# Padding three-row matmuls to 128 rows and shortening a routing step in an FFT and mixture-of-experts kernel

## The chip, the cores and the metric

The kernel runs on one core of a Trainium2 chip. A core has TensorE (PE in the rows; PEld is its weight load), VectorE (DVE), ScalarE (ACT), GpSimd (POOL) and SyncE (SP, which here only issues transfers). The metric is the device time of one execution in microseconds (us), the median over several runs.

## The reference, cut to what matters

```python
X = np.fft.fft(np.fft.fft(x, axis=1), axis=2).real        # x: 8 x 3072 x 256
x = X.reshape(8 * 3072, 256)
h = x @ w_in                                               # 256 -> 2048
g = h * np.clip(h + 3, 0, 6) / 6
x = g @ w_out                                              # 2048 -> 256
logits = x @ w_gate                                        # 8 experts
expert = argmax(logits); gate = softmax(logits)[expert]
out = gate * (relu(x @ w1[expert]) @ w2[expert])           # 256 -> 1024 -> 256
```

## The kernel before, in words

The transform over the 256 columns is folded into `w_in` when the kernel starts, and the one over the 3072 rows is done by folds on VectorE and GpSimd and by matmuls with tables. Because of symmetries, TensorE computes two halves, A and B, of each hidden tile; B - A and A + B are the hidden values of two mirrored sets of tokens. One column of the transform, d = 128, doesn't fit the 128 rows of a matmul. It enters by a matmul of its own with three rows (high part, low part and a cross term), whose weights are in the tile W3 and whose data are in q3.

The first stage has 48 chunks of 512 tokens, each with 8 steps (`step(s)`, 384 in all); a step is two hidden blocks of 128. In a step:

- `mm1` issues 6 matmuls for A, 2 three-row matmuls for d = 128 and 6 for B, into the tile `ab` (two banks; two such tiles take turns).
- `mm2` issues 24 matmuls of the step three before, 16 with gh and 8 with gl, into four banks `acc`.
- `h_of` copies A to SBUF on ScalarE and forms h[0] and h[1] on VectorE. Then come r (ScalarE), r times h (VectorE), gh (ScalarE) and gl (GpSimd) for the hidden values of the step before. r, gh and gl have four buffers of 512 each, two steps' worth.

At a chunk's end ScalarE evacuates acc (`evac`), and `routing` puts its stages into later steps: s0 and s1 find the expert, s2 counts on GpSimd, s3_mm computes the rank of each token by a matmul, s3 turns it into row numbers `pi` on VectorE, and s4 issues four scatters from GpSimd's queue, which write the tokens to DRAM in the order of experts. FFT matmuls of coming groups and folds of the next batch entry are put into the same steps by tables of step numbers. A batch entry has 6 chunks, 48 steps. The framework fixes each engine's order when the kernel is built, and each engine works strictly in its order.

After the first stage (from about 2162 us) the second mixture of experts works on tiles of 512 or 256 sorted tokens. The change doesn't touch that code.

`load_q3` copies rows of the transform to q3 by small SP transfers, three chunk steps before they are used.

Of the kernel before, what the change touches and what calls it, by code (L numbers as in the profile page):

```python
# [22 lines left out]
P = 128  # L23
# [32 lines left out]
QB = 5  # L56
BIG = float(1 << 20)
# [16 lines left out]
def tile_fft_moe(ctx, tc, xr, xf, xcoef, w_in, w_out, w_gate, w1, w2, tabs, fm, misc, tri, sgn8, dstc, maskc, out):  # L74
# [55 lines left out]
    sel1 = pc.tile([P, P], F32R, name="sel1")  # L130
# [7 lines left out]
    base8 = pc.tile([P, 4, NE], F32, name="base8")  # L138
# [191 lines left out]
    def load_q3(ci):  # L330
        b, g, c = chunks[ci]
        pq, o = gt[(b, g)], slice(c * 256, (c + 1) * 256)
        hold["q3", ci] = t = pw.tile([P, 256], F32R, tag="q3", name=f"q3_{ci}")
        v = t.rearrange("(j r) n -> j r n", r=32)
        for r, i in ((0, 2), (1, 2), (2, 3)):
            sp.dma_start(v[:, r].bitcast(F32), pq[0:1, i, None, o].to_broadcast([1, 4, 256]).bitcast(F32))
# [7 lines left out]
    def load_consts():  # L344
# [6 lines left out]
        sp.dma_start(base8, misc[:, o:o + 32].rearrange("p (a c) -> p a c", a=4))  # L351
        o += 32
# [5 lines left out]
    def start_tables():  # L358
        dve.memset(SS0.bitcast(F32), 0.0)
        for t in (XN, sel1):  # L360
            pool.memset(t.bitcast(F32), 0.0)
        dve.memset(half, 0.5)
        dve.memset(onesb, 1.0)
        dve.memset(sel1[0:1, :].bitcast(F32), 1.0)
        dve.memset(cnt, 0.0)

# [81 lines left out]
    def w_in_ev(c):  # L448
# [5 lines left out]
        th = pw.tile([P, 2, P], F32R, tag="Ac", name=f"th{c}")  # L454
        v = ab[:, :, 258:258 + P]
        act.activation(th, v, AF.Copy)
        for i in range(2):
            f = 2 * c + i
            r = slice(f % 4 * 32, f % 4 * 32 + 3)
            dve.scalar_tensor_tensor(out=W3[r, f // 4], in0=th[r, i], scalar=ssel[r, :], in1=v[r, i], op0=ALU.mult, op1=ALU.add)  # L460

# [25 lines left out]
    def mm1(ab, f0, pq, c0, q3):  # L487
        f = [slice((f0 + i) * P, (f0 + i + 1) * P) for i in range(2)]
        for i in range(2):
            for n, (a, c) in enumerate(PASS):  # L490
                pe.matmul(ab[:, i, 0:256], WA[a][:, f[i]], pq[:, c, c0:c0 + 256], start=n == 0, stop=False)  # L491
        for i in range(2):
            r = slice((f0 + i) % 4 * 32, (f0 + i) % 4 * 32 + 3)
            pe.matmul(ab[:, i, 0:256], W3[r, (f0 + i) // 4], q3[r], start=False, stop=True)  # L494
        for i in range(2):
            mm_group(ab[:, i, 256:512], [(WB[a][:, f[i]], pq[:, 2 + c, c0:c0 + 256]) for a, c in PASS])

    def h_of(ab, h, s):
# [47 lines left out]
    def routing(xo, xp, t0, nt, mask, tagn, wait=RKW):  # L546
# [5 lines left out]
        def s0():  # L552
# [4 lines left out]
            st["ex"] = ex = sm("rt_ex", [P, 4, NE])  # L557
            act.activation(ex[:, 0:nt], d[:, 0:nt], AF.Exp)
# [21 lines left out]
        def s3_mm():  # L580
            ab = hold["ride"][:, 1] if hold.get("ride") is not None else bank(f"rk{tagn}")
            st["r"] = r = ab[:, 384:384 + nt * NE]
            mm_group(r, [(trib, st["oh"][:, 0:nt].rearrange("p t e -> p (t e)")),
                         (onesb, st["oc"][:, 0:nt].rearrange("p t e -> p (t e)"))])

        def s3():
            k = st["k"]
            r = st["r"].rearrange("p (t e) -> p t e", e=NE)
            dve.tensor_tensor(out=k[:, 0:nt], in0=base8[:, 0:nt], in1=r, op=ALU.add)
            s = sm("rt_s", [P, 4])  # L590
            dve.tensor_reduce(out=s[:, 0:nt], in_=st["ex"][:, 0:nt], axis=AX.X, op=ALU.add)
# [690 lines left out]
```

## Time and profile before

| | |
|---|---|
| median of 3 runs | 3366.51 us (3363.07 to 3368.29) |
| the profiled execution | 3363.55 us; its span 3361.7 us |
| TensorE busy | 3207.4 us, 95% of the span |
| VectorE, ScalarE, GpSimd busy | 2277.2, 1939.8, 2263.8 us |
| first stage, second stage | about 44 to 2162 us, 2162 to 3361 us |

Matmuls are pipelined, so a busy share near 100% says that TensorE seldom stood still, not that each matmul was as short as it can be. What a matmul costs is read from the distance between starts. Waits name the instruction whose end came last.

### The profile page before, as it was taken

The numbers are of one execution on the slowest core, as the hardware profiler recorded it, in microseconds if no ns is written. First come the engines' busy times: TensorE is split into PE (matmuls) and PEld (weight loads), VectorE is DVE, ScalarE is ACT, GpSimd is POOL, SyncE is SP. The second block draws the span as 40 slices with busy tenths as digits, with TensorE's granted clock in tenths as the row PEclk, the third lists the DMA queues.
The fourth block names the chain that finished last, engine by engine and source line by source line (L and its number), as shares of the span: only waits on it lengthen the run. The fifth ranks groups of instructions, "written<-read, shape, count | busy, mean of one in ns | idle before, by whom it ended". The sixth has DMA issues, their size and how long they took to land.

```text
span 3361.7 us, 62365 instructions
## 1 busy us (share of the span) xinstructions
PE 3207.4 (95%) x23482; PEld 2983.5 (89%) x23482; DVE 2277.2 (68%) x3700; ACT 1939.8 (58%) x3339; POOL 2263.8 (67%) x1781
## 2 busy tenths in 40 slices
PE   5899999999999999999999999999999999999998
PEld 5899999889889889889889999888888888888887
DVE  8877777777777777777777665755555555555543
ACT  3566566566666666666666665645445444445453
POOL 5567776776776777677676775766666656666664
PEclk8999999999999999999999999999999999999999
DMA  5100100100100100000000001065555555555560
GB/s 180 61 28 19 38 24 16 43 24 16 39 27 16 33 33 16 33 31 18 27 14 16 14 16 50 20 180 159 153 151 152 151 146 148 159 147 154 146 170 31
DMA packets 248130, 243.45 MB, mean 72 GB/s; under 512 B 149099, under 2 KB 210956, under 8 KB 247824
## 3 DMA queue, kind: packets, MB, share of 16 engines
q1 hardware_dynamic: 226576, 184.94, 19.7%
q0 software_dynamic: 21248, 54.48, 4.5%
q8 instruction: 187, 3.06, 0.4%
q14 instruction: 119, 0.97, 0.1%
HBM read 159.71 MB, written 54.04 MB: 64 GB/s over the span
## 4 chain that ended last, share of the span: by engine, by line
PE 60%; ACT 13%; DVE 13%; issue 6%; POOL 2%; DMA 0%; SPq 0%; ACTq 0%; DVEq 0%; POOLq 0%
PE acc L517 16%; PE op L164 16%; PE hp L164 15%; PE ab L164 5%; ACT gh L961 5%; ACT r L505 5%; PE ab L491 4%; DVE h L183 2%; PE ab L494 2%; DVE r L512 1%; DVE R L188 1%; DVE R L180 1%; POOL gl L183 1%; DVE H L180 1%; DVE H L188 1%
## 5 line engine op out<-in xcount | busy, mean ns | idle before, releaser
L183 POOL TENSOR_TENSOR gl<-r,gh 128x512 fp32r<-128x512 f32 x768 | 1108.0, 1462 | 486.1 <-ACT gh L961 371.5
L505 ACT ACTIVATE r<-h,half 128x512 f32<-128x512 f32 x768 | 546.3, 719 | 590.3 <-DVE h L183 375.3
L512 DVE SCALAR_TENSOR_TENSOR r<-r,h 128x512 f32<-128x512 f32 x768 | 621.1, 813 | 363.2 <-ACT r L505 362.0
L517 PE MATMUL acc<-WO,gh 128*128 128x264 f32 x6144 | 822.7, 287 | 4.0 <-ACT xo L536 4.0
L517 PEld LDWEIGHTS acc<-WO,gh 128*128 128x128 f32 x6144 | 784.8, 191 | 4.2 <-ACT xo L536 4.2
L997 DVE SCALAR_TENSOR_TENSOR WB<-hp,WA 128x512 fp32r<-128x512 f32 (+1 forms) x472 | 278.8, 606 | 302.7 <-ACT WA L996 302.6
L961 ACT ACTIVATE gh<-r 128x512 fp32r<-128x512 f32 x768 | 450.9, 622 | 41.5 <-PE acc L517 14.7
L517 PE MATMUL acc<-WO,gl 128*128 128x264 f32 x3072 | 440.1, 285 | 0.5 <-POOL gl L183 0.5
L491 PE MATMUL ab<-pq,WA 128*128 128x256 f32 x2304 | 344.3, 285 | 64.2 <-DVE h L180 33.0
L517 PEld LDWEIGHTS acc<-WO,gl 128*128 128x128 f32 x3072 | 403.2, 189 | 0.9 <-POOL gl L183 0.9
L164 PE MATMUL ab<-pq,WB 128*128 128x256 f32 x2304 | 383.6, 303 | 0.0
L491 PEld LDWEIGHTS ab<-pq,WA 128*128 128x128 f32 x2304 | 300.6, 189 | 73.2 <-issue 53.9
L996 ACT ACTIVATE WA<-hp 128x512 fp32r<-128x512 f32 (+1 forms) x472 | 241.4, 531 | 197.6 <-PE hp L164 194.6
L164 PEld LDWEIGHTS ab<-pq,WB 128*128 128x128 f32 x2304 | 302.2, 192 | 50.4 <-issue 1.6
L148 POOL DMA_INDIRECT out_dram<-yo,dst x200 | 217.4, 1087 | 155.7 <-DVE yo L1097 117.7
L148 POOL DMA_INDIRECT xs_dram<-xp,pic x192 | 212.3, 1106 | 122.1 <-DVE pic L603 66.2
L164 PE MATMUL hp<-xTb,TB 128*128 128x512 f32 (+1 forms) x1344 | 277.3, 364 | 13.5 <-DVE WB L997 13.5
L164 PE MATMUL hp<-xTa,W1b 128*128 128x512 f32 (+1 forms) x1392 | 277.3, 358 | 3.2 <-DVE WB L997 3.2
L164 PEld LDWEIGHTS hp<-xTb,TB 128*128 128x128 f32 x1344 | 225.7, 188 | 57.8 <-DVE WB L997 15.3
L164 PE MATMUL op<-W2b,WA 128*128 128x256 f32 x1536 | 276.4, 282 | 0.0
L183 DVE TENSOR_TENSOR h<-A,ab 128x512 f32<-128x512 f32 x384 | 259.9, 677 | 22.1 <-ACT A L500 21.6
L164 PEld LDWEIGHTS hp<-xTa,W1b 128*128 128x128 f32 x1392 | 228.9, 189 | 44.4 <-DVE WB L997 3.6
(268 smaller groups left out, 5328.0 us busy)
## 6 DMA issues: line engine op xcount, KB each, us to landing
w1a<-in_w_dram SPq DMA_DIRECT2D x29, 1024.0 KB
w1b<-in_w_dram SPq DMA_DIRECT2D x29, 1024.0 KB
w2b<-in_w_dram SPq DMA_DIRECT2D x58, 512.0 KB
R<-in_xr_dram SPq DMA_DIRECT2D x32, 774.0 KB
w2a<-in_w_dram SPq DMA_DIRECT2D x29, 768.0 KB
w2d<-in_w_dram SPq DMA_DIRECT2D x28, 256.0 KB
raw<-in_w_in_dram SPq DMA_DIRECT2D x8, 512.0 KB
rawo<-in_w_out_dram SPq DMA_DIRECT2D x8, 512.0 KB
```

The lines of the kernel that those rows point to most:

```text
L148: i = pool.indirect_dma_start(oob_is_err=False, **kw)
L164: pe.matmul(dst, l, r, start=(n == 0), stop=(n == len(terms) - 1))
L180: pinned(eng.tensor_tensor(out=o, in0=a, in1=b, op=ALU.add))
L183: i = eng.tensor_tensor(out=o, in0=a, in1=b, op=ALU.subtract)
L188: pinned(dve.scalar_tensor_tensor(out=o, in0=a, scalar=s, in1=b, op0=ALU.mult, op1=ALU.add))
L491: pe.matmul(ab[:, i, 0:256], WA[a][:, f[i]], pq[:, c, c0:c0 + 256], start=n == 0, stop=False)
L505: act.activation(r, h, AF.Relu, bias=half, scale=1.0 / 6.0)
L512: dve.scalar_tensor_tensor(out=g, in0=r, scalar=1.0, in1=h, op0=ALU.min, op1=ALU.mult)
L517: pe.matmul(acc[t][:, 0:GW], lhs, wo(w, f0 + i), start=st, stop=sp_)
L961: act.activation(gh[n], g[n], AF.Copy)
L996: act.activation(hi, ps, AF.Relu)
L997: dve.scalar_tensor_tensor(out=lo, in0=ps, scalar=0.0, in1=hi, op0=ALU.max, op1=ALU.subtract)
```

## The change

The three-row matmuls become matmuls of 128 rows. The weights of W3 move into rows 32 to 34 (first block of a step) and 64 to 66 (second block) of the tile XN, whose rows 0 to 15 hold other weights. q3 becomes two static tiles, one for odd and one for even chunks, zeroed once; its two halves have data only in rows 32 to 34 and only in rows 64 to 66. Each of these matmuls now directly follows its block's three A matmuls. A of both blocks goes to the first bank of ab and B to the second, where before each bank had A and B of one block. `load_q3` issues six transfers a chunk where it issued three.

In routing the base of each expert's rows is added by a third rank matmul (its values are 32 more columns of the tile trib); the 1e-9 of the softmax sum is a constant ninth column that the sum takes in; the sum over experts writes integers itself, so the cast goes; the copy of the destination rows moves from VectorE to ScalarE. Without a mask s3 has 4 VectorE instructions instead of 8.

```diff
-    W3 = pc.tile([P, KF // 4, P], F32R, name="W3")
-    trib = pc.tile([P, P], BF16, name="trib")
-    XN = pc.tile([P, X_W], F32R, name="XN")
+    trib = pc.tile([P, P + 4 * NE], BF16, name="trib")
+    ex9s = {n: pc.tile([P, n, NE + 1], F32, name=f"ex{n}") for n in (4, 1)}
+    XN = pc.tile([P, 8 * P], F32R, name="XN")
+    q3 = [pc.tile([P, 2, 256], F32R, name=f"q3{n}") for n in range(2)]
...
         for r, i in ((0, 2), (1, 2), (2, 3)):
-            sp.dma_start(v[:, r].bitcast(F32), pq[0:1, i, None, o].to_broadcast([1, 4, 256]).bitcast(F32))
+            for n in range(2):
+                sp.dma_start(q3[ci % 2][32 * n + 32 + r:32 * n + 33 + r, n].bitcast(F32), pq[0:1, i, o].bitcast(F32))
...
-        for t in (XN, sel1):
+        for t in (XN, *q3):
             pool.memset(t.bitcast(F32), 0.0)
...
-    def mm1(ab, f0, pq, c0, q3):
+    def mm1(ab, f0, pq, c0, q):
         f = [slice((f0 + i) * P, (f0 + i + 1) * P) for i in range(2)]
+        w = XN[:, f0 // 2 * P:(f0 // 2 + 1) * P]
         for i in range(2):
-            for n, (a, c) in enumerate(PASS):
-                pe.matmul(ab[:, i, 0:256], WA[a][:, f[i]], pq[:, c, c0:c0 + 256], start=n == 0, stop=False)
+            mm_group(ab[:, 0, i * 256:(i + 1) * 256], [(WA[a][:, f[i]], pq[:, c, c0:c0 + 256]) for a, c in PASS] + [(w, q[:, i])])
         for i in range(2):
-            r = slice((f0 + i) % 4 * 32, (f0 + i) % 4 * 32 + 3)
-            pe.matmul(ab[:, i, 0:256], W3[r, (f0 + i) // 4], q3[r], start=False, stop=True)
-        for i in range(2):
-            mm_group(ab[:, i, 256:512], [(WB[a][:, f[i]], pq[:, 2 + c, c0:c0 + 256]) for a, c in PASS])
+            mm_group(ab[:, 1, i * 256:(i + 1) * 256], [(WB[a][:, f[i]], pq[:, 2 + c, c0:c0 + 256]) for a, c in PASS])
...
-            act.activation(ex[:, 0:nt], d[:, 0:nt], AF.Exp)
+            act.activation(ex9s[nt][:, :, 0:NE], d[:, 0:nt], AF.Exp)
+            act.activation(xp.bitcast(F32)[:, 0:nt, D + 1:XW], dst_sb[:, t0:t0 + nt, None].to_broadcast([P, nt, XW - D - 1]), AF.Copy)
...
-                         (onesb, st["oc"][:, 0:nt].rearrange("p t e -> p (t e)"))])
+                         (onesb, st["oc"][:, 0:nt].rearrange("p t e -> p (t e)")),
+                         (onesb, trib[:, P:P + nt * NE])])
...
-            dve.tensor_tensor(out=k[:, 0:nt], in0=base8[:, 0:nt], in1=r, op=ALU.add)
+            dve.tensor_tensor(out=k[:, 0:nt], in0=r, in1=st["oh"][:, 0:nt], op=ALU.mult)
+            ps = pi if mask is None else sm("rt_p", [P, 4])
+                dve.tensor_reduce(out=ps[:, 0:nt], in_=k[:, 0:nt], axis=AX.X, op=ALU.add)
-            dve.tensor_reduce(out=s[:, 0:nt], in_=st["ex"][:, 0:nt], axis=AX.X, op=ALU.add)
-            dve.tensor_tensor(out=k[:, 0:nt], in0=k[:, 0:nt], in1=st["oh"][:, 0:nt], op=ALU.mult)
-            dve.tensor_scalar(s[:, 0:nt], s[:, 0:nt], 1e-9, None, op0=ALU.add)
-            dve.tensor_reduce(out=ps[:, 0:nt], in_=k[:, 0:nt], axis=AX.X, op=ALU.add)
+            dve.tensor_reduce(out=s[:, 0:nt], in_=ex9s[nt], axis=AX.X, op=ALU.add)
...
-            dve.tensor_copy(xp.bitcast(F32)[:, 0:nt, D + 1:XW], dst_sb[:, t0:t0 + nt, None].to_broadcast([P, nt, XW - D - 1]))
-            dve.tensor_copy(pi[:, 0:nt], ps[:, 0:nt])
```

The framework's order moves with it. On VectorE, in the fourth step of the fourth batch entry's second chunk (step 155), the rows from the read of the rank to the row numbers are these before; f_1_1 is the bank in which the rank matmul's result lies, rt_kc a scratch tile of the routing, and pic the row numbers `pi`.

```order
1193 L589 TENSOR_TENSOR rt_kc_11257<-base_103,f_1_1_11624 128x32
1194 L183 TENSOR_TENSOR h_0_11729<-A_11731,ab_11686 128x512
1195 L592 TENSOR_TENSOR rt_kc_11257<-rt_kc_11257,rt_ohc_11261 128x32
1196 L180 TENSOR_TENSOR h_1_11730<-A_11731,ab_11686 128x512
1197 L177 SCALAR_TENSOR_TENSOR pq_1_11058<-pf_1_1_11669,pq_1_11058 128x512
1198 L595 TENSOR_REDUCE rt_pc_11680<-rt_kc_11257 128x4
1199 L512 SCALAR_TENSOR_TENSOR r_0_11804<-r_0_11804,h_0_11729 128x512
1200 L603 CAST pic_11683<-rt_pc_11680 128x4
1201 L512 SCALAR_TENSOR_TENSOR r_1_11805<-r_1_11805,h_1_11730 128x512
```

The same place of the changed kernel, on VectorE:

```order
1123 L587 TENSOR_TENSOR rt_kc_11232<-f_1_1_11601,rt_ohc_11236 128x32
1124 L185 TENSOR_TENSOR h_0_11702<-A_11704,ab_11659 128x512
1125 L591 TENSOR_REDUCE pic_11654<-rt_kc_11232 128x4
1126 L182 TENSOR_TENSOR h_1_11703<-A_11704,ab_11659 128x512
1127 L179 SCALAR_TENSOR_TENSOR pq_1_11037<-pf_1_1_11647,pq_1_11037 128x512
1128 L560 SCALAR_TENSOR_TENSOR rt_kc_11795<-rt_dc_11727,iom_105 128x32
1129 L509 SCALAR_TENSOR_TENSOR r_0_11777<-r_0_11777,h_0_11702 128x512
1130 L509 SCALAR_TENSOR_TENSOR r_1_11778<-r_1_11778,h_1_11703 128x512
```

The row numbers stood seven places behind the read of the rank and now stand two behind it.

On GpSimd, around the scatters (DMA xs_dram) of the same chunk, the order before is this:

```order
501 L575 COPY rt_occ_11892<-cnt 128x8
502 L183 TENSOR_TENSOR gl_0_11739<-r_0_11735,gh_0_11737 128x512
503 L183 TENSOR_TENSOR gl_1_11740<-r_1_11736,gh_1_11738 128x512
504 L148 DMA xs_dram<-xp_11096,pic_11683 198656x260 x4
505 L183 TENSOR_TENSOR gl_0_11808<-r_0_11804,gh_0_11806 128x512
```

The same place of the changed kernel, on GpSimd:

```order
510 L572 COPY rt_occ_11865<-cnt 128x8
511 L150 DMA xs_dram<-xp_11076,pic_11654 198656x260
512 L185 TENSOR_TENSOR gl_0_11712<-r_0_11708,gh_0_11710 128x512
513 L185 TENSOR_TENSOR gl_1_11713<-r_1_11709,gh_1_11711 128x512
514 L150 DMA xs_dram<-xp_11076,pic_11654 198656x260 x3
515 L185 TENSOR_TENSOR gl_0_11781<-r_0_11777,gh_0_11779 128x512
```

The first of the four scatters has moved ahead of a pair of gl. This is so in 28 of the 48 chunks; in the others all four stay together.

## Rows read from the trace of the kernel before

**Rows 1.** Busy time by stretch of the span, two stretches, us
```profile
core 0: us, PE busy (x) PEld busy (x) DVE busy (x) ACT busy (x) POOL busy (x), PEclk, DMA share, GB/s
353.00:1875.00 1522.00, 1462.05 (x11328) 1373.76 (x11327) 1172.34 (x1935) 975.11 (x1792) 1090.68 (x982) 0.99 0.08 26
1875.00:2095.00 220.00, 220.00 (x1707) 207.07 (x1706) 137.66 (x266) 139.75 (x254) 145.66 (x129) 0.98 0.10 28
```

**Rows 2.** Three-row matmuls (line 494, two a step) in four stretches; count in brackets
```profile
1875.00:2095.00 220.00, 15.35 (x80) 7.38 (x80) 0.98 0.10 28
353.00:1875.00 1522.00, 108.83 (x564) 52.32 (x564) 0.99 0.08 26
165.00:353.00 188.00, 14.00 (x72) 6.75 (x72) 0.98 0.07 22
44.00:165.00 121.00, 5.19 (x24) 2.52 (x24) 0.82 0.21 68
```

**Rows 3.** Timeline of TensorE, one step: start us, us of the merged group
```profile
1004.20 0.87 PE L491 MATMUL ab<-pq,WA 128*128 128x256 f32 x6
1004.99 0.39 PE L494 MATMUL ab<-q,W 3*128 3x256 f32 x2
1005.31 0.97 PE L164 MATMUL ab<-pq,WB 128*128 128x256 f32 x6
1006.12 2.10 PE L517 MATMUL acc<-WO,gh 128*128 128x264 f32 x16
...
1009.05 0.87 PE L491 MATMUL ab<-pq,WA 128*128 128x256 f32 x6
```

**Rows 4.** Line 491: duration ns min/median/max
```profile
L491 PE MATMUL ab<-pq,WA x2304: 274/279/522, 44.3 to 2162.1; 128*128 128x256 f32 x192
```

**Rows 5.** Waits of TensorE, 353 to 1875 us: total us, times, longest
```profile
PE ab L491 <- DVE h L180: 29.5, 31, 2.0
PE ab L491 <- DVE rt_kc L589: 22.3, 22, 1.7
```

**Rows 6.** Waits of ScalarE, 353 to 1875 us
```profile
ACT r L505 <- DVE h L183: 292.7, 160, 3.6
ACT r L505 <- POOL gl L183: 158.1, 61, 3.8
```

**Rows 7.** Waits of GpSimd, 353 to 1875 us
```profile
POOL xs_dram L148 <- DVE pic L603: 55.6, 23, 4.1
...
POOL xs_dram L148 <- DVE rt_kc L563: 5.4, 6, 0.9
```

**Rows 8.** Timeline of VectorE around step 155
```profile
942.49 1.14 DVE L592 TENSOR_TENSOR rt_kc<-rt_kc,rt_ohc 128x32 f32<-128x32 f32 x1
...
945.29 0.17 DVE L595 TENSOR_REDUCE rt_pc<-rt_kc 128x4 f32<-128x32 f32 x1
...
945.99 0.15 DVE L603 CAST pic<-rt_pc 128x4 int32<-128x4 f32 x1
```

**Rows 9.** Timeline of GpSimd, the same place
```profile
942.29 2.53 POOL L183 TENSOR_TENSOR gl<-r,gh 128x512 fp32r<-128x512 f32 x2 [2.75 <-ACT gh L961]
946.42 1.22 POOL L148 DMA_INDIRECT xs_dram<-xp,pic  x1 [1.60 <-DVE pic L603]
947.94 0.98 POOL L148 DMA_INDIRECT xs_dram<-xp,pic  x1 [0.30 <-issue]
...
952.30 2.54 POOL L183 TENSOR_TENSOR gl<-r,gh 128x512 fp32r<-128x512 f32 x2
```

**Rows 10.** Timeline of ScalarE, the same place
```profile
953.62 0.73 ACT L505 ACTIVATE r<-h,half 128x512 f32<-128x512 f32 x1 [3.77 <-POOL gl L183]
```

**Rows 11.** The chain that ended last, 150 to 2165 us, shares by line
```profile
by line: PE acc L517 27.2%; issue 9.1%; PE ab L164 9.0%; ACT gh L961 8.3%; ACT r L505 7.9%; PE ab L491 7.4%; DVE h L183 4.0%; PE ab L494 3.1%; DVE r L512 2.3%; DVE R L188 2.3%; DVE R L180 2.2%; POOL gl L183 1.9%; DVE H L180 1.8%; DVE H L188
```

**Rows 12.** Groups by line, 870 to 1129 us, one batch entry
```profile
L558 ACT ACTIVATE rt_exc<-rt_dc 128x32 f32<-128x32 f32 x6 | 1.5, 254 | 0.0
```

**Rows 13.** Timeline of GpSimd at the start
```profile
0.74 0.84 POOL L361 MEMSET XN<- 128x896 f32 x1 [0.29 <-POOLq L1270]
```

More of the change, by code (lines that the diff above doesn't have):

```diff
@@ L56 @@
 QB = 5
+AB = 2
 BIG = float(1 << 20)
@@ L363, in start_tables @@
         dve.memset(onesb, 1.0)
-        dve.memset(sel1[0:1, :].bitcast(F32), 1.0)
         dve.memset(cnt, 0.0)
+        for t in ex9s.values():
+            dve.memset(t, 1e-9)
     def load_tables():
@@ L457, in w_in_ev @@
         for i in range(2):
-            f = 2 * c + i
-            r = slice(f % 4 * 32, f % 4 * 32 + 3)
-            dve.scalar_tensor_tensor(out=W3[r, f // 4], in0=th[r, i], scalar=ssel[r, :], in1=v[r, i], op0=ALU.mult, op1=ALU.add)
+            r = slice(32 * i + 32, 32 * i + 35)
+            dve.scalar_tensor_tensor(out=XN[r, c * P:(c + 1) * P], in0=th[r, i], scalar=ssel[r, :], in1=v[r, i], op0=ALU.mult, op1=ALU.add)
     def start_wg():
@@ L588, in s3 @@
             r = st["r"].rearrange("p (t e) -> p t e", e=NE)
-            dve.tensor_tensor(out=k[:, 0:nt], in0=base8[:, 0:nt], in1=r, op=ALU.add)
-            s = sm("rt_s", [P, 4])
-            dve.tensor_reduce(out=s[:, 0:nt], in_=st["ex"][:, 0:nt], axis=AX.X, op=ALU.add)
-            dve.tensor_tensor(out=k[:, 0:nt], in0=k[:, 0:nt], in1=st["oh"][:, 0:nt], op=ALU.mult)
-            dve.tensor_scalar(s[:, 0:nt], s[:, 0:nt], 1e-9, None, op0=ALU.add)
-            ps = sm("rt_p", [P, 4])
-            dve.tensor_reduce(out=ps[:, 0:nt], in_=k[:, 0:nt], axis=AX.X, op=ALU.add)
+            dve.tensor_tensor(out=k[:, 0:nt], in0=r, in1=st["oh"][:, 0:nt], op=ALU.mult)
+            st["pi"] = pi = pw.tile([P, 4], I32, tag=f"rt_pi{nt}", name=f"pi{tagn}")
+            ps = pi if mask is None else sm("rt_p", [P, 4])
+            with nc.allow_low_precision(reason="one term of the sum is not zero, and all are whole"):
+                dve.tensor_reduce(out=ps[:, 0:nt], in_=k[:, 0:nt], axis=AX.X, op=ALU.add)
+            s = sm("rt_s", [P, 4])
+            dve.tensor_reduce(out=s[:, 0:nt], in_=ex9s[nt], axis=AX.X, op=ALU.add)
             dve.reciprocal(xp.bitcast(F32)[:, 0:nt, D], s[:, 0:nt])
@@ L599, in s3 @@
                                          op0=ALU.mult, op1=ALU.add)
[L600 to L603 removed]
+                dve.tensor_scalar(pi[:, 0:nt], ps[:, 0:nt], BIG, None, op0=ALU.add)
         def s4(t):
@@ L935, in step @@
                 ab = ab_tile(f"ab{s}")
-                mm1(ab, f0, gt[(b, g)], c * 256, hold["q3", s // STEPS])
+                mm1(ab, f0, gt[(b, g)], c * 256, q3[s // STEPS % 2])
             hold["ride"] = None
@@ L1183, in _constants @@
     misc = np.concatenate(cols, 1)
-    tri = (p[:, None] < p[None, :]).astype(float)
+    base = np.tile(np.arange(8.0) * CAPR + TS, 4)
+    parts = np.zeros((P, 32))
+    parts[0] = base // 8192 * 8192
+    parts[1] = base % 8192
+    assert (parts % 256 == 0).all()
+    tri = np.concatenate([(p[:, None] < p[None, :]).astype(float), parts], 1)
     sgn8 = np.where(p[None, :, None] // 2 == np.arange(NB)[:, None, None], (-1.0) ** n, 0.0)
```

29 lines of the change are left out of this document (11 added, 18 removed).

## The prediction

> **What bounds the kernel now.** I read the busy time by stretch first, then one step of TensorE instruction by instruction, then the waits of each engine. The change touches the first stage alone, so the second stage, from 2162 us on, counts as unchanged.
>
> The first stage has stretches of two kinds. From 1875 to 2095 us, where the folds have ended, TensorE is busy for 220.00 of 220.00 us [rows 1] over 40 steps (80 three-row matmuls, two a step [rows 2]): TensorE sets the end there. From 353 to 1875 us, 282 steps, it is busy for 1462.05 of 1522.00 us, and it looks like the bound. But it stands still when VectorE's h or the read of the rank is late (29.5 and 22.3 us [rows 5]), and each such stop says that in that chunk the other engines came last. Their ring is: A copied (ScalarE), h (VectorE), r (ScalarE), r times h (VectorE), gh (ScalarE), gl (GpSimd). Within it ScalarE's r waits 292.7 us for h and 158.1 us for gl [rows 6], since r may not overwrite a buffer that gl still reads. GpSimd in turn is late with gl because four scatters stand ahead of it, and these wait 55.6 + 5.4 = 61.0 us for routing on VectorE [rows 7]. So in these 35 chunks a faster TensorE first waits longer, and what moves the time is mainly the ring.
>
> **The padded matmuls.** A full matmul of 256 columns: six A matmuls take 0.87 us from first start to last end, one of them lasts 0.279 us [rows 3, 4], so starts are (0.87 - 0.28) / 5 = 0.118 us apart. The 14 matmuls of one `mm1` go from 1004.20 to 1006.12, 1.92 us [rows 3]. At 0.118 us each they would take 1.65 us. The three-row pair therefore costs 0.27 us more than two full matmuls would: last A start at 1004.79, pair at 1004.99, B at 1005.31 [rows 3], so 0.20 us pass ahead of the pair and 0.32 us behind its start. The two of the pair start together (0.39 us for both). After the change all 14 are alike in shape, and I take 0.118 us for each of the two new ones. At worst the gaps come from something else and stay, then each pair costs one slot more than now (+0.12 us); that is a rival below.
>
> The Trainium skill speaks against this edit: "TensorE: Matmul & The Clock Gate", Part 3, says that matmuls with few rows in different row groups run at the same time, and that this is what small row counts gain. By that rule the pair would cost one slot, its padded form two, and 384 steps would lose 384 x 0.118 = 45 us if TensorE were the bound throughout. The trace agrees that the two run together, but the 0.20 and 0.32 us around them outweigh it; the measurement decides.
>
> On TensorE this is 384 x 0.27 = 104 us in all. What of it moves the end, by stretch [rows 2]:
> - 1875 to 2095 us: 40 steps x 0.27 = 10.8 us, in full, as TensorE never waits there. The third rank matmul of 32 columns isn't in the trace; it costs between 0 and 0.12 us (a full one), so at most 0.6 us in five chunks. I take 10.2 us.
> - 353 to 1875 us: 282 x 0.27 = 76 us are there. I count none of it as a term of its own, because the ring must move first (next part); the 0.27 us a step only keep TensorE from becoming the new bound, 8 x 0.27 = 2.2 us a chunk.
> - 165 to 353 us: 36 steps, between 0 and 9.7 us. The stretch has both kinds of chunk; half, 4.9 us.
> - 44 to 165 us: 12 steps, where weights are still converted, and the last 14 steps: 0 to 3.2 and 0 to 3.8 us. I take 1.5 us each.
>
> **Routing and the ring.** In the chunk around 942 us the row numbers are ready at 945.99 + 0.15 = 946.14 and the first scatter starts at 946.42, after GpSimd waited 1.60 us [rows 8, 9]. In the new order the reduction that writes them stands where the multiplication at 942.49 stands now. With its 0.17 us it ends at 942.66, 3.5 us earlier. The first scatter now comes ahead of gl: start 942.66 + 0.28 = 942.94, 0.98 us, then the gl pair, 2.53 us, then three scatters with 0.30 us between them [rows 9]: 942.94 + 0.98 + 2.53 + 3 x 1.28 = 950.29, where the next gl starts at 952.30 now. That is 2.0 us earlier. ScalarE's r at 953.62 waited 3.77 us for just this gl [rows 10], so it can take all of it, and TensorE gains 2.2 us a chunk to follow.
>
> Other chunks differ. Where the four scatters stay behind gl, the gain is the whole wait for the row numbers; where the first one is moved ahead of gl and gl could have started sooner than here, the moved scatter holds gl up and part is lost. The bounds are 0 and the whole 61.0 us of these waits [rows 7]. The one chunk worked out lies above the mean wait (61.0 / 35 = 1.74 us), the chunks with an early gl below it, and I take a little over half, 33 us.
>
> What else leaves VectorE (the sum with the base, the 1e-9, the cast, the copy) lies in time in which ScalarE waits for GpSimd anyway, so I add nothing; if that cover goes, four instructions of some 0.17 us, as the reduction [rows 8], would be 0.7 us a chunk more, which the upper bound of 61.0 us leaves room for. The copy of the destination rows on ScalarE costs about as much as the small exponential beside it, 0.25 us a chunk [rows 12]. It stands between A and gh; as r waits for GpSimd two steps later, it is hidden, and costs at most 48 x 0.25 = 12 us if that wait is gone. The six transfers a chunk in place of three stand on SP's queue with three steps, over 14 us, to land before their matmuls; queued behind them are only loads of the folds, asked for six steps ahead. Zero cost, and should they be late, TensorE waits at a chunk's first step.
>
> At the start GpSimd zeroes 1024 columns more, at 0.84 us for 896 [rows 13] about 1 us, ahead of the loads of the tables. I take 0.5 us lost.
>
> The changed banks gain nothing: A's copy still waits for the last B matmul of its step, whose end alone is signalled.
>
> **The sum.** 10.2 + 4.9 + 1.5 + 1.5 + 33 - 0.5 = 50.6 us. The profiled execution took 3363.55 us, of which 3361.7 us is the span; 3363.55 - 50.6 = 3313 us. It lies 3 us below the median of the runs shown, so 3366.5 - 50.6 = 3316 us for the median. As a check: line 494 has 3.1% of the chain from 150 to 2165 us [rows 11], 62.5 us; a pair holds 0.32 us of it, so some 195 of the pairs lie on the chain, and 195 x 0.27 = 53 us. The chain counts some of them where a scatter in fact came last, so it is no proof, but the size agrees.
>
> **The rivals.**
> - *TensorE is the bound all along.* The stops [rows 5] would be just short waits, and all 384 steps give 0.27 us: 3366.5 - 104 = 3262 us. For it: 95% busy. Against it: the waits of 158.1 and 292.7 us in the ring [rows 6]. Some more could come on top if the ring gets faster than I think. Chance 0.15.
> - *The ring doesn't move.* Only the stretches count in which TensorE is the bound: 10.2 + 4.9 + 3.0 - 0.5 = 17.6 us, 3349 us. For it: in many chunks VectorE's folds, not GpSimd, make h late (292.7 us [rows 6]). Chance 0.15.
> - *The moved scatter holds up gl: slower.* In 28 chunks the first scatter stands ahead of gl and GpSimd works strictly in order. By the sum above, the next gl starts 7.63 us after the row numbers are ready; with 952.30 us as the break-even they must be ready by 944.67. If the reduction were no earlier than the cast is now (946.14), the next gl would start at 953.77, 1.5 us later, and 28 chunks would lose 41 us: 3366.5 - 17.6 + 41 = 3390 us. Against it: the reduction has only one h between it and the read of the rank. Chance 0.05.
> - *The gaps stay.* By the concurrency rule alone, or if the 0.20 and 0.32 us come from the turn from A to B and not from the three rows, each step gains one slot and loses nothing: 40 + 18 + 13 steps on the bound x 0.12 = 8.5 us slower there, and half of the ring's gain can still be had, which TensorE then can't follow in all chunks: about 3366.5 + 8.5 - 10 = 3365 us. The skill's "TensorEngine Tiling (Array Packing)", Key Properties, says that a change of tiling mode drains the engine, which would explain the gaps by the three rows; no run here has shown it yet. Chance 0.05.
>
> **How the numbers follow.** The forecast, 3316 us, has 0.60; its own range, from 20 to 80 us gained, is 3286 to 3346 us. The range for 8 in 10 reaches halfway to the TensorE rival and down to the case of the standing ring: 3278 to 3350 us. No change within 0.2% (6.7 us, about what three runs of this kernel can tell) is left to the fourth rival and a weak second: 0.05; slower by more 0.06; faster 0.89.
>
> **What the profile would show.** Right: the B matmuls follow A without a gap, `mm1` in 1.65 us; scatters start some 3 us earlier in the chunk; r's wait for gl falls from 158 us toward 100; TensorE's stops grow, because it gains more than the ring. Wrong: r's wait for gl grows (the third rival), gaps around the new matmuls (the fourth), or TensorE without stops in all chunks (the first).

## The result and the profile after

The change made the kernel slower: 3396.53 us (median of 4 runs, 3395.26 to 3401.37) against 3366.93 us for the kernel before on the same chip, ratio 1.0092 [1.0076, 1.0108]. Forecast were 3316 us, with 0.06 for slower. The profiled execution took 3401.37 us, its span 3399.5 us.

Busy time of the changed kernel in the first stretch of [rows 1]:

```profile
core 0: us, PE busy (x) PEld busy (x) DVE busy (x) ACT busy (x) POOL busy (x), PEclk, DMA share, GB/s
353.00:1875.00 1522.00, 1374.11 (x10974) 1343.14 (x10973) 1211.02 (x1733) 937.77 (x1759) 1042.24 (x952) 0.99 0.08 25
```

From 353 to 1875 us VectorE ran 202 instructions fewer than before (1733 against 1935) and was busy 38.7 us longer; TensorE did fewer matmuls in the same time. The granted clock is 0.99 in both, so it explains nothing. The loss has one place. From the first A matmul of chunk 6 to that of chunk 42, six batch entries, it is 1604.2 us (352.9 to 1957.1) against 1551.9 (355.7 to 1907.6) before: 52.3 us lost. Ahead of chunk 6 the change gained 2.8 us, and from chunk 42 to the first matmul of the last step 12.6 us (241.3 against 253.9).

TensorE, one step, to be read beside [rows 3]:

```profile
1006.92 0.55 PE L166 MATMUL ab<-pq,WA 128*128 128x256 f32 x3
1007.32 0.28 PE L166 MATMUL ab<-q,XN 128*128 128x256 f32 x1
1007.43 0.52 PE L166 MATMUL ab<-pq,WA 128*128 128x256 f32 x3
1007.79 0.28 PE L166 MATMUL ab<-q,XN 128*128 128x256 f32 x1
1007.91 0.88 PE L166 MATMUL ab<-pq,WB 128*128 128x256 f32 x6
1008.63 2.10 PE L514 MATMUL acc<-WO,gh 128*128 128x264 f32 x16
```

The gaps around the pair are gone: `mm1` goes from 1006.92 to 1008.63, 1.71 us, where it took 1.92 and 1.65 were forecast. Over all steps the median from its first start to its last end fell from 2.10 to 1.84 us. The padded matmul did its part; the loss lies elsewhere.

Waits from 353 to 1875 us, the lines that answer to [rows 5 to 7]:

```profile
ACT r L502 <- DVE h L185: 420.3, 198, 5.1
...
PE ab L166 <- DVE h L182: 84.9, 84, 2.2
...
ACT gh L958 <- DVE r L509: 42.0, 18, 2.5
ACT r L502 <- POOL gl L185: 36.5, 11, 3.5
POOL xs_dram L150 <- ACT pq L178: 35.5, 12, 3.4
POOL xs_dram L150 <- DVE pic L591: 35.0, 11, 3.9
...
POOL xs_dram L150 <- DVE rt_kc L560: 15.8, 5, 3.2
```

r's wait for gl fell much further than forecast (36.5 us, 158.1 before). The scatters don't wait less for the row numbers, though the line that names them is smaller (35.0 us, 55.6 before). In all 34 chunks of the stretch the first scatter starts 0.28 us behind the end of the row numbers, whichever engine the wait is put down to, and these waits are 92.2 us in all, against 61.0 in [rows 7]. And r's wait for h rose by 127.6 us, to 420.3, TensorE's by 55.4, and gh now waits for VectorE's r times h. VectorE has become late. Where it loses is seen in the groups of its instructions from 353 to 1875 us (behind the x the count, then busy us and the mean ns of one):

```profile
L509 DVE SCALAR_TENSOR_TENSOR r<-r,h 128x512 f32<-128x512 f32 x545 | 435.5, 805 | 241.8 <-ACT r L502 239.1 <-ACT gh L958 1.7 <-issue 0.6
...
L185 DVE TENSOR_TENSOR h<-A,ab 128x512 f32<-128x512 f32 x272 | 183.3, 674 | 0.0
...
L560 DVE SCALAR_TENSOR_TENSOR rt_kc<-rt_dc,iom 128x32 f32<-128x32 f32 x34 | 37.5, 1104 | 0.0
...
L567 DVE TENSOR_TENSOR rt_ohc<-rt_ohc,msk_sb 128x32 bf16<-128x32 bf16 x6 | 19.1, 3176 | 0.2 <-DVE xp L594 0.2
```

A 128x32 multiplication (line 560) takes 1104 ns on average here and took 179 in the kernel before; the masked one (line 567) 3176 ns against 193. h, one of whose inputs lies in PSUM, takes 674 ns, where it took 676. One chunk shows why. It is step 155 again, VectorE's timeline:

```profile
961.93 0.18 DVE L591 TENSOR_REDUCE pic<-rt_kc 128x4 int32<-128x32 f32 x1
962.03 0.68 DVE L182 TENSOR_TENSOR h<-A,ab 128x512 f32<-128x512 f32 x1
962.62 0.68 DVE L179 SCALAR_TENSOR_TENSOR pq<-pf,pq 128x512 fp32r<-128x512 f32 x1
963.22 2.80 DVE L560 SCALAR_TENSOR_TENSOR rt_kc<-rt_dc,iom 128x32 f32<-128x32 f32 x1
965.94 1.28 DVE L509 SCALAR_TENSOR_TENSOR r<-r,h 128x512 f32<-128x512 f32 x2
...
969.45 3.21 DVE L567 TENSOR_TENSOR rt_ohc<-rt_ohc,msk_sb 128x32 bf16<-128x32 bf16 x1
972.59 1.28 DVE L509 SCALAR_TENSOR_TENSOR r<-r,h 128x512 f32<-128x512 f32 x2
```

GpSimd's, the same place, to be read beside [rows 9]:

```profile
962.39 1.01 POOL L150 DMA_INDIRECT xs_dram<-xp,pic  x1 [3.42 <-ACT pq L178]
963.41 2.55 POOL L185 TENSOR_TENSOR gl<-r,gh 128x512 fp32r<-128x512 f32 x2
...
970.06 2.55 POOL L185 TENSOR_TENSOR gl<-r,gh 128x512 fp32r<-128x512 f32 x2
```

ScalarE's next gh then waits for r times h:

```profile
966.71 1.24 ACT L958 ACTIVATE gh<-r 128x512 fp32r<-128x512 f32 x2 [2.21 <-DVE r L509]
```

The small multiplication at 963.22 ends at 966.02, and the gl pair at 965.96; the masked one at 969.45 ends at 972.66, and the next pair at 972.61. The two r times h stand behind them on VectorE. gl has two inputs in SBUF, and so have the instructions that stretch. The Trainium skill ("SBUF — State Buffer", Who interferes with whom) says that a VectorE instruction with two SBUF inputs contends with a GpSimd instruction that reads SBUF; the same page (Summary: rules for kernel authors) says that the second one to issue blocks until the first is done. The trace agrees that such instructions are held and h isn't, but not that one GpSimd instruction sets the length: both of these were held through two gl, and from 0.19 and 0.61 us ahead of the first one's record on. What the long holds have in common was counted over the traces from 353 to 1875 us (r times h, the fold into pq and routing's small multiplications). In the kernel before, each of the some 190 instructions that a gl pair holds is held by one GpSimd operation, at most some 1.2 us beyond its own time. Where the pair follows a scatter without a pause, and the instruction starts in the last 0.6 us of the scatter's record or behind it, ahead of the first gl, it is held through both gl, 2.53 to 3.06 us: 24 in the changed kernel (once with a small tensor operation between scatter and pair). In the kernel before VectorE comes to such a pair only during its second gl (23 times, some 0.35 us each). The moved scatter set up this meeting. The runs below widen the condition: behind a scatter, 56 more instructions that started only during the first gl (11 in `pin_s1`, 17 in `spread`, 28 in `pad_spread`) were held to the end of the second. With no scatter before the pair, over 1500 instructions of the runs that keep gl were held from a start ahead of its second gl, and none of them beyond the first.

### The profile page after: what moved, and what is told of

Same layout as the page of the kernel before. It is cut to its first block, busy times and chain, and to the rows that moved or that the text cites. A ratio compares the mean times of both kernels' runs of the same rounds, so it can differ in the third digit from the quotient of the medians.

```text
span 3399.5 us, 62598 instructions
## 1 busy us (share of the span) xinstructions
PE 3140.8 (92%) x23531; PEld 3000.0 (88%) x23531; DVE 2347.6 (69%) x3505; ACT 1936.2 (57%) x3388; POOL 2254.8 (66%) x1784
## 5 line engine op out<-in xcount | busy, mean ns | idle before, releaser
L166 PE MATMUL ab<-pq,WA 128*128 128x256 f32 x2304 | 401.0, 290 | 141.5 <-DVE h L182 95.1
L166 PEld LDWEIGHTS ab<-pq,WA 128*128 128x128 f32 x2304 | 331.3, 191 | 164.1 <-issue 120.6
L166 PE MATMUL ab<-pq,WB 128*128 128x256 f32 x2304 | 348.1, 287 | 0.0
L166 PEld LDWEIGHTS ab<-pq,WB 128*128 128x128 f32 x2304 | 310.6, 194 | 0.0
```

Source lines behind the costliest of these rows:

```text
L166: pe.matmul(dst, l, r, start=(n == 0), stop=(n == len(terms) - 1))
```

## The experiments

Three theories stood at the start. **Held**: the new order puts gl pairs, now behind a scatter, where VectorE has instructions with two SBUF inputs, and each is held for up to a whole pair. **Late**: gl itself comes later behind the moved scatter, and r and TensorE's `mm2` wait for it, whatever VectorE does. **Padding**: the padded matmuls, their banks or the six transfers cost time. In the table, "entry" is the time of one batch entry, a sixth of that from chunk 6 to chunk 42; "held" counts VectorE's instructions in that stretch that last over 2 us longer than undisturbed. Both are worked out from each trace. Each ratio is to the kernel before on the same chip. `pin_s1`, `behind`, `pin_cast`, `spread`, `pad_spread`, `late_gl4`, `before_gl1`, `after_gl1`, `pad_fold` and `behind_fold` came out outside every range expected for them; only the difference between `before_gl1` and `after_gl1`, 95 to 110 us expected, came true.

| run | median us | ratio | entry us | held |
|---|---|---|---|---|
| before | 3366.5 | 1 | 258.7 | 0 |
| the change | 3396.53 | 1.0092 [1.0076, 1.0108] | 267.4 | 42 |
| pad_only | 3347.37 | 0.9946 [0.9930, 0.9963] | 258.9 | 0 |
| route_only | 3414.42 | 1.0142 [1.0125, 1.0159] | 267.4 | 41 |
| cast_kept | 3349.64 | 0.9949 [0.9932, 0.9965] | 259.3 | 6 |
| pin_s1 | 3404.29 | 1.0113 [1.0096, 1.0130] | 267.6 | 43 |
| behind | 3357.83 | 0.9976 [0.9967, 0.9986] | 260.3 | 0 |
| pin_cast | 3361.04 | 0.9990 [0.9980, 1.0000] | 260.6 | 17 |
| gap | 3381.89 | 1.0043 [1.0028, 1.0057] | 264.2 | 0 |
| spread | 3416.48 | 1.0148 [1.0131, 1.0165] | 267.0 | 40 |
| pad_spread | 3432.09 | 1.0194 [1.0177, 1.0211] | 269.2 | 51 |
| late_gl4 | 3444.00 | 1.0231 [1.0214, 1.0248] | 273.5 | 0 |
| before_gl1 | 3258.88 | 0.9695 [0.9678, 0.9711] | 244.5 | 0 |
| after_gl1 | 3157.25 | 0.9383 [0.9367, 0.9399] | 231.7 | 0 |
| pad_dst | 3346.73 | 0.9955 [0.9938, 0.9971] | 259.1 | 0 |
| pad_fold | 3254.54 | 0.9668 [0.9652, 0.9684] | 244.4 | 42 |
| after_fold | 3258.31 | 0.9683 [0.9667, 0.9699] | 243.8 | 53 |
| behind_fold | 3237.36 | 0.9616 [0.9600, 0.9632] | 240.5 | 16 |

**The two halves.** `pad_only` has the padded matmuls, their banks and the six transfers, with routing as before; `route_only` has the new routing with the three-row matmuls.

```diff
 pad_only, against the change:
-            dve.tensor_tensor(out=k[:, 0:nt], in0=r, in1=st["oh"][:, 0:nt], op=ALU.mult)
+            dve.tensor_tensor(out=k[:, 0:nt], in0=base8[:, 0:nt], in1=r, op=ALU.add)
...
 route_only, against the change:
-            mm_group(ab[:, 0, i * 256:(i + 1) * 256], [(WA[a][:, f[i]], pq[:, c, c0:c0 + 256]) for a, c in PASS] + [(w, q[:, i])])
+            pe.matmul(ab[:, i, 0:256], W3[r, (f0 + i) // 4], q3[r], start=False, stop=True)
```

> Padded matmuls, changed banks and six q3 transfers, routing as before: the order of VectorE and GpSimd is that of before. Theory A (the new order of VectorE and GpSimd makes the ring slower, since VectorE's instructions with two SBUF inputs are held while a gl pair runs): faster than before by 17 to 45 us, 3322 to 3350 us; mean of rt_kc from rt_dc stays near 0.18 us. Theory B (the faster TensorE by itself puts the ring into a worse phase): slower than before, 3375 to 3410 us, with the long VectorE waits here too.

> Routing changed, three-row matmuls as before: the order of VectorE and GpSimd is that of the changed kernel. Theory A: slower than the changed kernel by what TensorE gives it outside the ring, 3405 to 3425 us; rt_kc from rt_dc takes about 1 us in the mean. Theory B: 3350 to 3367 us, no long VectorE waits.

`pad_only` gained 19.2 us and `route_only` lost 47.8. Their sum, 28.6, is the change's own loss (29.6): the halves add up, and **padding** is refuted as the cause. In the ring stretch padding gained nothing (258.9 us an entry against 258.7), though TensorE needs less there:

```profile
353.00:1875.00 1522.00, 1400.63 (x11308) 1377.31 (x11307) 1170.02 (x1933) 971.31 (x1791) 1091.75 (x983) 0.99 0.08 25
```

It is busy 61.4 us less than in [rows 1] and stands still instead: its waits for h and for the read of the rank grew from 29.5 and 22.3 us [rows 5] to 60.1 and 31.4.

**Which part of the routing.** `cast_kept` writes the row numbers by a cast of their own; that is one VectorE instruction more than in the change, and keeps all four scatters together in 37 of the 48 chunks, where the traces show 36 in the kernel before and 17 in the change (27 of its chunks have a whole gl pair behind the first scatter, and 4 a single gl, so in three of the 20 chunks that were said to keep all four together they are split). `pin_s1` keeps the multiplication of line 560 where the program has it, behind h of the next step, and leaves the scatters early. `pin_cast` does both. `behind` leaves VectorE's and ScalarE's order as in the change, and only has GpSimd copy one value of gl into a column of `xp` that nothing reads, ahead of the scatters, so that these must follow the gl pair.

```diff
 cast_kept:
-            ps = pi if mask is None else sm("rt_p", [P, 4])
+            ps = sm("rt_p", [P, 4])
+            if mask is None:
+                dve.tensor_copy(pi[:, 0:nt], ps[:, 0:nt])
 pin_s1:
+            tc.keep_in_program_order(dve.scalar_tensor_tensor(out=k[:, 0:nt], in0=st["d"][:, 0:nt], ...
 behind:
+            if nt == 4 and hold["gl"] and t == 0:
+                pool.tensor_copy(xp.bitcast(F32)[:, 0:4, XW - 1:XW], hold["gl"][1][:, 0, 0:4, None].bitcast(F32))
```

> The changed kernel with the cast of the row numbers kept as an instruction of its own: all four scatters stand behind the gl pair again in nearly all chunks, while rt_kc from rt_dc still stands ahead of r times h. Theory S (the scatter moved ahead of gl is the loss, by holding gl up or by making the gl pair run back to back): 3320 to 3350 us. Theory K (the early place of rt_kc from rt_dc is the loss): stays at 3385 to 3400 us.

> The changed kernel with rt_kc from rt_dc kept at its place in program order, which puts it behind h in the next step, as before; the first scatter still stands ahead of gl. Theory K: rt_kc from rt_dc falls from 1.05 to about 0.2 us in the mean, 3340 to 3365 us. Theory S: 3385 to 3400 us.

> The changed kernel with one tiny GpSimd copy that makes all four scatters of a chunk wait for the gl pair of their step; the copied value goes into a column of the scattered rows that nothing reads. VectorE's and ScalarE's order is that of the changed kernel, row for row; only the scatters move behind gl. Theory S (the scatter ahead of gl is the loss): 3340 to 3355 us, rt_kc from rt_dc at 0.2 us in the mean. If VectorE's order has a part in it: 3365 to 3396 us.

> The changed kernel with the cast kept and rt_kc from rt_dc at its place in program order, so that scatters and rt_kc both stand as before, with four fewer... three fewer VectorE instructions a chunk. If the order is all that matters: within 8 us of pad_only, 3340 to 3352 us; if the routing instructions left out are worth something by themselves: 3320 to 3338 us.

Of the 49.2 us by which the change lies above `pad_only`, `behind` gets back 38.7 merely by keeping the scatters behind gl, with one more GpSimd instruction, and `cast_kept` 46.9. `behind` lies between the two ranges expected for it, so the rest, some 10 us, may be VectorE's new order or the added instruction. `pin_cast`, with the scatters as in `cast_kept`, is 13.7 us above `pad_only` and has 17 long holds: all 17 are at a pair that follows three or four scatters in a row, so a long hold doesn't need a scatter moved ahead of gl. `pin_s1` gets back nothing: line 560 has a mean of 179 ns again, but 43 other instructions are held instead (r times h has a mean of 885 ns, the masked one of 2113). So it isn't a particular VectorE instruction that was badly moved, but the scatter ahead of the gl pair. Step 155 in `behind`, VectorE in the same order as above:

```profile
945.50 0.68 DVE L182 TENSOR_TENSOR h<-A,ab 128x512 f32<-128x512 f32 x1
946.10 1.06 DVE L179 SCALAR_TENSOR_TENSOR pq<-pf,pq 128x512 fp32r<-128x512 f32 x1
947.08 1.27 DVE L560 SCALAR_TENSOR_TENSOR rt_kc<-rt_dc,iom 128x32 f32<-128x32 f32 x1
948.27 1.28 DVE L509 SCALAR_TENSOR_TENSOR r<-r,h 128x512 f32<-128x512 f32 x2
...
951.78 0.16 DVE L567 TENSOR_TENSOR rt_ohc<-rt_ohc,msk_sb 128x32 bf16<-128x32 bf16 x1
951.86 1.29 DVE L509 SCALAR_TENSOR_TENSOR r<-r,h 128x512 f32<-128x512 f32 x2
```

GpSimd in `behind`, the same place:

```profile
945.31 2.99 POOL L185 TENSOR_TENSOR gl<-r,gh 128x512 fp32r<-128x512 f32 x2 [2.86 <-ACT gh L961]
948.37 0.64 POOL L602 COPY xp<-gl 128x4 f32<-128x4 f32 x1
949.28 1.17 POOL L150 DMA_INDIRECT xs_dram<-xp,pic  x1 [0.28 <-POOL xp L602]
950.76 0.97 POOL L150 DMA_INDIRECT xs_dram<-xp,pic  x1 [0.30 <-issue]
952.04 1.35 POOL L150 DMA_INDIRECT xs_dram<-xp,pic  x1 [0.30 <-issue]
953.70 1.17 POOL L150 DMA_INDIRECT xs_dram<-xp,pic  x1 [0.30 <-issue]
954.89 2.54 POOL L185 TENSOR_TENSOR gl<-r,gh 128x512 fp32r<-128x512 f32 x2
```

The pair begins while VectorE computes h, which it doesn't hold. The fold at 946.10 is held by the first gl only (1.06 us in place of 0.68), line 560 by the second only (it ends at 948.35, the pair at 948.30). The masked multiplication takes 0.16 us, not 3.21, and the r times h behind it run at full speed beside a scatter (1.29 us for two): four scatters in a row are a window without gl for VectorE.

**Breaking the pair, and other places for the scatters.** `gap` puts a copy of one column between the two gl in two steps of a chunk, where the scatters then land. `spread` puts one scatter behind each of four gl pairs; `pad_spread` does so without the new routing.

```diff
 gap:
                 for n in range(2):
+                    if n and s % STEPS in (3, 4):
+                        pool.tensor_copy(gl[1][:, 0, 0:1], gl[0][:, 0, 0:1])
                     sub(pool, gl[n], g[n], gh[n])
 spread, pad_spread, for each t of the four:
+                pool.tensor_copy(xp.bitcast(F32)[:, t, XW - 1:XW], hold["gl"][1][:, 0, 0:1].bitcast(F32))
```

> The changed kernel with a copy of one column between the two gl of a pair, in two steps of each chunk; the framework then also puts a scatter or two between them, so the second gl comes later than in the changed kernel, but the pair no longer runs back to back. VectorE's order is unchanged. Port theory (VectorE's instruction with two SBUF inputs waits until a back-to-back pair is through): rt_kc from rt_dc and the masked rt_ohc stay under 1.6 us, 3350 to 3385 us. Hold theory (gl comes late because scatters stand ahead of it): slower than the changed kernel, 3400 to 3440 us.

> The changed kernel with each scatter of a chunk tied to the gl pair of a step of its own: one scatter behind each of four pairs in place of four in a row. VectorE's order is unchanged. If the wait of r for gl (98 to 158 us where the four stand together) is on the ring: that wait falls below 40 us and a batch entry takes less than 254 us in place of 259, 3300 to 3325 us. If VectorE's folds set the ring: the wait moves to h, 3335 to 3355 us.

> The same spreading of the scatters with the padded matmuls alone and routing as before. As for spread: 3300 to 3325 us if the wait for gl is on the ring, 3335 to 3350 us if VectorE's folds set it. The difference to spread is what the shorter routing is worth once the scatters stand in the same places: 0 to 10 us.

`gap` makes the second gl later still, which by **late** costs more; it was 14.6 us faster than the change, and none of its instructions is held over 2 us beyond its own time. VectorE in `gap`:

```profile
777.90 2.24 DVE L190 SCALAR_TENSOR_TENSOR H<-H 128x258 f32<-128x258 f32 x1
780.06 0.18 DVE L560 SCALAR_TENSOR_TENSOR rt_kc<-rt_dc,iom 128x32 f32<-128x32 f32 x1
780.16 0.68 DVE L509 SCALAR_TENSOR_TENSOR r<-r,h 128x512 f32<-128x512 f32 x1
...
780.86 1.68 DVE L509 SCALAR_TENSOR_TENSOR r<-r,h 128x512 f32<-128x512 f32 x1
```

GpSimd, the same place:

```profile
778.51 1.33 POOL L185 TENSOR_TENSOR gl<-r,gh 128x512 fp32r<-128x512 f32 x1
779.90 0.27 POOL L961 CAST gl<-gl 128x1 fp32r<-128x1 f32 x1
780.26 1.73 POOL L185 TENSOR_TENSOR gl<-r,gh 128x512 fp32r<-128x512 f32 x1
```

The first gl here follows a scatter, and the fold that starts 0.61 us ahead of it is held through it, as in the change; but it ends at 780.14 (the gl at 779.84). With the copy behind that gl the hold doesn't go on through the second: two instructions run at full speed in the break, and the next one is held by the second gl (1.68 us for 0.68). `spread` doesn't bear out a guess of my own: that a smaller wait of r for gl (158.1 us, [rows 6]) is a gain. With the scatters apart it fell to 24 us, and the kernel was slower than the change, 3416.48 us, and so it was with the old routing (`pad_spread`, 84.7 us over `pad_only`). But each scatter now stands in front of a pair, with 40 and 51 long holds (6 of the 51 are of an instruction with one input), so these runs don't price the wait by itself.

**A shorter gl.** gl is one copy of gh, with one input, in both kernels; the low part of the gated values is left out, so the times say only what gl costs.

```diff
-                    sub(pool, gl[n], g[n], gh[n])
+                    pool.tensor_copy(gl[n], gh[n])
```

> The kernel before with gl as a plain GpSimd copy of gh: one input from SBUF in place of two; the low part of the gated values is left out, so its output is not the reference's. The order of every engine stays, row for row. Port theory (VectorE's instructions with two SBUF inputs wait for a GpSimd instruction that reads two): no VectorE instruction is held any more, the folds take 0.4 to 0.95 us each, TensorE becomes the bound in all chunks: 248 to 251 us a batch entry, 3295 to 3320 us. If a copy holds VectorE just as long for its own duration: folds still over 1.2 us, above 3335 us.

> The changed kernel with the same copy in place of gl (same part left out), its order unchanged, scatters ahead of gl included. Port theory: the early scatter costs nothing any more and TensorE is the bound, so the padded matmuls give their whole 0.27 us a step: 95 to 110 us below before_gl1, 3190 to 3225 us. If the early scatter costs by holding gl up: not over 60 us below before_gl1.

Both are faster by over 100 us, and the order turns: the change is now 101.6 us faster than the kernel before. That is the 384 x 0.27 = 104 us of the whole padding, and where TensorE is the bound the early scatter costs nothing measurable. From 353 to 1800 us TensorE never stands in `before_gl1` and `after_gl1`, in this order:

```profile
353.00:1800.00 1447.00, 1447.00 (x11406) 1367.28 (x11405) 1016.80 (x1952) 1000.54 (x1803) 617.47 (x988) 1.00 0.08 27
```
```profile
353.00:1800.00 1447.00, 1447.00 (x12072) 1442.87 (x12071) 1063.30 (x1890) 1052.44 (x1933) 659.46 (x1038) 1.00 0.08 27
```

This doesn't tell **held** from **late**, since the copy takes 0.65 us and shortens both, and the copies still hold VectorE (line 560 has a mean of 633 ns in `after_gl1`). It does show that gl's time is what the ring hangs on.

**gl late without a scatter, and the copy on ScalarE.** `late_gl4` is `pad_only` with the gl pairs of four of the eight steps tied to the later gh, so that both gl start later and follow each other directly. `pad_dst` is `pad_only` with the copy of the destination rows on ScalarE.

```diff
 late_gl4:
+                if s % STEPS in (0, 3, 5, 7):
+                    pool.tensor_copy(gl[0][:, 0, 0:1], gh[1][:, 0, 0:1])
                 for n in range(2):
                     sub(pool, gl[n], g[n], gh[n])
 pad_dst:
+            act.activation(xp.bitcast(F32)[:, 0:nt, D + 1:XW], dst_sb[:, t0:t0 + nt, None].to_broadcast([P, nt, XW - D - 1]), AF.Copy)
```

> pad_only with the gl pairs of four of the eight steps tied to the later gh: both gl then run back to back, the first of them about 0.5 us later, with no scatter moved. Theory H (what costs is that VectorE is held through a back-to-back pair, whatever stands ahead of it): VectorE instructions of over 2 us appear, 3360 to 3410 us. Theory G (what costs is gl itself coming late, by a scatter of 1 us and more): 0.5 us fits into the slack, 3343 to 3353 us, no VectorE instruction over 2.1 us.

> pad_only with the copy of the destination rows on ScalarE, as in the changed kernel; the order of the scatters and of rt_kc is that of before. I counted this edit at nothing: 3343 to 3351 us. If ScalarE's 0.25 us a chunk stands on the ring: 3352 to 3360 us.

`late_gl4` was meant to decide, and decided only half. It is the slowest run, so late pairs cost much with no scatter moved ahead; but VectorE meets no pair behind a scatter before its second gl, and no instruction is held over 2 us beyond its own time (r times h has a mean of 893 ns, so many are held by one gl). Two of its waits for gl from 353 to 1800 us, and the same two of `pad_only`:

```profile
ACT r L502 <- POOL gl L185: 161.1, 54, 5.3
...
PE acc L514 <- POOL gl L185: 33.6, 73, 0.8
```
```profile
ACT r L502 <- POOL gl L185: 133.8, 46, 4.0
...
PE acc L514 <- POOL gl L185: 1.4, 7, 0.2
```

So **late** looks like a cost of its own when gl is late enough: TensorE waits for it. In the change it is not the one that shows: r's wait for gl fell to 36.5 us there. `pad_dst` is level with `pad_only`: the copy is hidden.

**The folds.** VectorE's lateness suggested a version: its folds, with two SBUF inputs, stand ahead of h. Three kernels issue them right behind h of the same step, with h kept in that place: `pad_fold`, `after_fold` and `behind_fold`, made from `pad_only`, the change and `behind`.

```diff
-                fill[u0 + n].append(lambda f=f: in_order(f))
+                hfill[u0 + n].append(lambda f=f: in_order(f))
...
-                h_of(ab, h, s)
+                in_order(lambda: h_of(ab, h, s))
+                for f in hfill.pop(s, []):
+                    f()
```

> pad_only with the fold instructions of VectorE moved from behind r times h to behind h of the same step, where gl of the step before has ended. If the folds that gl holds up are what sets the ring: they take 0.4 to 0.95 us again, a batch entry falls from 259 to 240 to 250 us, 3265 to 3315 us, although the scatters stand earlier again in 20 chunks. If the ring is set by something else (ScalarE's chain, the wait for gl): 3335 to 3355 us.

> The changed kernel with the folds moved in the same way, scatters ahead of gl in 30 chunks. Theory H: the folds' part is won, the hold by the early scatter stays: 20 to 50 us above behind_fold.

> The kernel behind (changed kernel, all four scatters behind the gl pair) with the folds moved in the same way. Theory H: like pad_fold or up to 15 us faster, since no scatter stands ahead of gl and routing is shorter, 3255 to 3305 us. Otherwise 3345 to 3360 us.

The folds' place is worth 92.8 us on `pad_only`, 120.5 on `behind` and 138.2 on the change. `behind_fold` is the fastest version that leaves nothing out, some 130 us below the kernel before. It is 21.0 us faster than `after_fold`, which is what the early scatters still cost. It is 17.2 faster than `pad_fold`, too, but that doesn't show that the new routing has a value: the scatters of `pad_fold` are split in 37 chunks, those of `behind_fold` in none. Its waits from 353 to 1800 us:

```profile
ACT r L502 <- DVE h L185: 221.5, 177, 2.6
ACT r L502 <- POOL gl L185: 191.3, 83, 6.1
...
PE ab L166 <- DVE h L182: 1.3, 5, 0.3
```

TensorE's stops for h are gone.

## Why the prediction was wrong

**What bounds the kernel: half right.** That the ring, not TensorE, sets the pace from 353 to 1875 us is shown by `pad_only` (nothing gained there) and, from the other side, by `before_gl1`. But I read the ring by its waits alone, and a smaller wait of r for gl as a gain.

**The padded matmuls: right.** 0.27 us a step where TensorE is the bound: 101.6 of 104 us between the two kernels with a short gl. Outside the ring the terms were 10.2 + 4.9 + 1.5 + 1.5 - 0.5 = 17.6 us; `pad_only` measured 19.2. The rival "the ring doesn't move" (3349 us) comes within 2 us of that kernel's 3347.37.

**Routing and the ring: the step that failed.** The term of 33 us gained was a loss of 48 (`route_only`). On GpSimd the working came true in step 155: from the read of the rank on, the row numbers end 3.5 us earlier than before, as worked out, the first scatter follows 0.28 us later, and the next gl pair starts 1.7 us earlier (2.0 forecast). Yet the scatters' waits, from which the 33 us were taken, didn't shrink (92.2 us, 61.0 before), since a scatter ahead of gl waits where gl used to run. What failed is "then the gl pair, 2.53 us, then three scatters": I moved GpSimd's instructions in time and kept every duration. VectorE's durations aren't constants beside gl. The sign stood in my own rows: in [rows 8] the multiplication at 942.49 took 1.14 us, and the reduction on the same 128x32 data 0.17; the gl pair of [rows 9] began at 942.29. I used the 0.17 and didn't ask about the 1.14.

**The rival "the moved scatter holds up gl": right place, right sign, wrong mechanism, chance too small.** It gave 3390 us. Its condition, row numbers no earlier than the cast, was not met, and r's wait for gl, its mark, fell; that its 3390 us lies near the measured 3396.53 is luck. The moved scatter did harm with early row numbers, and as step 155 and the waits show it, through VectorE: gl is moved onto r times h and routing's small instructions. `behind`, which takes back that one move, gets 38.7 us back.

**The costs put at nothing: right for the copy** on ScalarE (`pad_dst`). The banks and the six transfers weren't tried alone; with the padding they leave no loss. Less VectorE work gained nothing either: `cast_kept`, with the scatters together about as often as before and fewer instructions, is level with `pad_only`. At the start the first step begins 2.6 us later (46.9 against 44.3 us) where 0.5 were forecast. That it comes from the change isn't shown: `before_gl1`, whose start is that of the kernel before, begins at 46.5.

**The chances.** 0.89 for faster rested on terms of which all but the start's 0.5 us could only gain. No rival priced a VectorE instruction that becomes slower. The signs named for being right came true (no gaps around the new matmuls, r's wait for gl down, TensorE's stops for h up from 29.5 to 84.9 us) while the kernel became slower: none of them looked at VectorE.

**What stays open.** How the 48 us divide. 42 instructions held for some 2.8 us are 118 us of VectorE's time, and 52 us show at the end; how much of that hides, and how much of the loss is gl coming late, isn't settled. For **held** speak the counts (with the folds in their old place 0 to 17 where the scatters stand as before or behind gl, 40 to 51 where one stands ahead of a whole pair), step 155, and `gap`. But `gap` got back only 14.6 us without a long hold, `pin_cast` has 17 and lies within 0.1% of the kernel before, `late_gl4` lost 97 us to `pad_only` without one, and `pad_fold` bears 42: the count alone doesn't give the time. The sum comes nearer. Over all of VectorE's instructions, short holds included, the time beyond the shortest of each one's kind is 44 us an entry in the kernel before and in `pad_only`, 45 in `behind`, 47 in `cast_kept`, 53 in `pin_cast`, 57 in `gap`, 59 in the change, 61 in `spread` and 64 in `pad_spread`, nearly the order of their times. So `gap` broke up the long holds but kept nearly all of the held time. `late_gl4`, with 54, is far slower than this order would have it; there gl's lateness counts. An order of this kind is no proof of a cause.

## What to carry to other kernels

When a change moves a GpSimd instruction, a scatter too, look at what VectorE does at that moment: in these traces an instruction with two SBUF inputs beside a gl takes its own time plus about what is left of that gl, while one with an input in PSUM or a reduction does not. Two instructions of one shape with different durations in a trace are the sign; ask what ran beside the slower one before using either. A wait that shrinks is not a gain by itself: ask what the other engines do in that time, and what takes its place.

## What the runs showed of the hardware

A VectorE instruction with two SBUF inputs that comes to two GpSimd operations in a row is held by one of them (at most some 1.2 us beyond its own time in the kernel before), but until both are done (2.5 to 3.1 us in the change) when a scatter stands directly before the first and the instruction starts ahead of the second. In `gap`, with a copy of one column (0.27 us) between the two, the hold ended with the first. Why a scatter makes the difference no run shows. h, with an input in PSUM, never took over 0.7 us from 353 to 2162 us in any run. One input in SBUF is no safeguard: six times in `pad_spread` a 128x4 tensor_scalar of 0.15 us took some 3.0 us. A scatter that another scatter follows holds nothing (0.64 us each for r times h beside one). And a pair of three-row matmuls, which start together, costs 0.27 us more than two with 128 rows; the banks were regrouped with the padding, and neither was tried alone.
